# ScalarE takes the ordering reads, GpSimd all sums of the seventh and eighth tile, with new offsets in the planner

## The chip, the core and the metric

The kernel runs on one core of one Trainium2 chip, in one launch. The metric is device microseconds of one execution, as a median over runs. The core has TensorE (PE, the matrix engine), VectorE (DVE), ScalarE (ACT), GpSimd (POOL) and the queue engine SP, which issues most of the DMAs. Every engine works through its own queue strictly in order and waits on semaphores for what the others make.

## The reference

Two stages follow each other: a linear attention with decay in blocks of 64 positions, and a feed-forward layer with the gate h·cos(h).

```python
for b in range(nb):                                   # 12 blocks of 64
    intra = einsum('bhic,bhjc->bhij', qb, kb) * Dmask
    intra = einsum('bhij,bhjd->bhid', intra, vb)
    inter = einsum('bhid,bhde->bhie', qb * lam_pow, kv_state)
    out[:, :, sl] = intra + inter
    kv_state = lam_block * kv_state + einsum('bhsd,bhse->bhde', kb * rev_pow, vb)
x = out.transpose(0, 2, 1, 3).reshape(3072, 512)
h = x @ w_in                                          # 512 -> 2048
return (h * cos(h)) @ w_out                           # 2048 -> 512
```

Batch 4, 8 heads, 768 positions, head dimension 64; so the second stage has 3072 rows, which are 24 blocks of 128.

## The kernel before, in words

The 24 blocks are taken in pairs `pr`. The first two pairs (the spans) have a form of their own and make the lead of the kernel; each of the other ten pairs has one **visit** to TensorE: `add_scores` and `add_stretch` put down the scores (L458), the update of the state (L470), a first group of value matmuls (`values`, L521) and a second group with the carried state (`values_carried`, L521 and L553). Where two visits are joined, the scores and the update of the next pair stand between the two groups of values of this one. The two groups write into the same PSUM tiles from different row halves of the array; so that they are taken in turn, a one-element copy out of PSUM (`turn`, L538, seven of them) reads what the first group wrote, and the first matmul of the second group depends on it by hand (L547).

The feed-forward layer goes by nine tiles of 4, 2, 2, 2, 2, 4, 2, 2 and 4 blocks (`TILES`). For each slice of the hidden layer TensorE makes h (L828, or L1030 in the first four tiles), ScalarE its cosine (L834, L1036) and VectorE the product g (L837, L1042). The last five tiles (`FAST`, the fifth to the ninth) use a product scheme with seven instead of eight partial products; for that five sums of parts of g are made for each half of the slices (`combine`, L858, L860, L861: names 5, 2, 1, 7 and 6 for the halves 0 and 1, ten for a tile), and five sums of parts of w_out once (L786, on GpSimd, in twenty pieces, each held back until the values of a block named in `SLOT` are scaled). The products of a tile (L912, L909) run while the hidden layer of the next tile is made, and in the order of `SEQ`: for the first two blocks of a tile 5, 2, 3, 4, 1 of half 0, then 3, 4, 5, 2, 1 of half 1, then 7 and 6. The products 3 and 4 need no sum. VectorE joins the partial products to the output (L936, L946, L979), and SP stores it.

No order is written out by hand: a **planner** (`Planner.order`) places each task at build time, by given durations, latencies and buffers. On each engine it takes, of the tasks that could start first, the one with the smallest `prio`, and emits them in that order. A task with `worth` may be taken ahead of others although it could start that much later. `prio` is a due time: `begins` and `unit` are the planned starts and lengths of the tiles (`ATT` is what is added to them for each block), `LATER` moves the visits of a pair, `HASTE` the masks of the scores (L463) of pairs from 8 on, `CMB` and `CMBT` the sums of g (the latter by tile and half). `ON` names, for each tile, the engine of its ten sums: five of half 0, then five of half 1.

GpSimd also scales q and v (L380, L388) and casts k (L384) of all later blocks, as the loads land; SP then transposes q and k by DMA (L416).

Of the kernel before, what the change touches and what calls it, by code (L numbers as in the profile page):

```python
# [20 lines left out]
SPLIT = 5  # L21
BANKS = 8
LAG = 2
ATT = 0.95
LOAD_US = 1.22
ALONE = [3, 4, 8]
WF = ["ACT", "POOL", "ACT", "POOL"]
# [2 lines left out]
HELD = (10,) * 12  # L30
FAST = [4, 5, 6, 7, 8]
TILES = [4, 2, 2, 2, 2, 4, 2, 2, 4]
CMB = (-3.0, 5.0, -1.0)
HASTE = 10
CMBT = [(0.0, 0.0), (0.0, 0.0), (0.0, 0.0), (0.0, 0.0), (12.0, 12.0), (-12.0, -12.0), (16.0, 34.0), (0.0, -18.0), (6.0, -16.0)]
LATER = {3: 7.0, 4: -2.0, 5: -8.0, 6: -8.0, 7: -2.0, 8: 14.0, 9: 7.0, 10: 10.0, 11: 4.0}
KACT = ()
ON = ['DDDDDDDDDD', 'DDDDDDDDDD', 'DDDDDDDDDD', 'DDDDDDDDDD', 'DDDDDDDDDD', 'DDDDDDDDDD', 'PPPPPDDDDD', 'PPPPPDDDDD', 'DDDDDDDDDD']
SLOT = [5, 6, 6, 7, 8, 9, 9, 10, 10, 11, 11, 11, 12, 12, 12, 13, 13, 14, 15, 16]
WSUM = [(x, "POOL", 2, 70.0) for x in ("11+22", "12-22", "21-11", "21+22", "11+12")]  # L40
SEQ = [[(n, (g,)) for g, x in enumerate(("52341", "34521")) for n in x] + [(n, (0, 1)) for n in "76"], [(n, (0, 1)) for n in "5234176"]]

# [138 lines left out]
def kernel(  # L181
# [10 lines left out]
    nc = tc.nc  # L192
    B, H, S, D = q.shape
# [3 lines left out]
    NP = H // 2  # L197
# [55 lines left out]
    spare = consts.tile([P, 112], F32)  # L253
# [7 lines left out]
    pl = Planner({**BUFS, "q_f": BUFS["ld"], "k_f": BUFS["ld"], "v_f": BUFS["ld"]})  # L261
# [4 lines left out]
    live = {}  # L266

    HF, HM = KF // 2, DM // 2
    QF = HF // 2
    unit = [MM(n * P, 4 * KF) + (MM(HM, 7 * HF * n // 2) if i in FAST else MM(DM, KF * n)) + ATT * n for i, n in enumerate(TILES)]  # L270
    begins = [sum(unit[:i]) for i in range(len(unit) + 1)]

    def prio_attn(n, part):
        i = next(i for i in range(len(TILES)) if n < first[i + 1])
        return begins[i - 1] + unit[i - 1] * (n - n % 2 - first[i] + 2 * part) / TILES[i]
# [87 lines left out]
    def tile_of(n):  # L363
        return next((i, n - first[i]) for i in range(len(TILES)) if n < first[i + 1])
# [80 lines left out]
    def add_scores(pr, part):  # L445
# [38 lines left out]
        for s in range(2):  # L484
            So[n0 + s] = pl.add("DVE", 0.69, [s_t] + ([So[n0]] if s else []), partial(scores_out, s=s), pa(0.25 + 0.1 * s) - (HASTE if pr >= 8 else 0.0), get="s_m")
        s_t.bank_frees = [[So[n0]], [So[n0 + 1]]]
# [21 lines left out]
    def add_stretch(pr, ahead=None):  # L508


        n0 = 2 * pr
        g, c = divmod(pr, NB)
        pa = lambda part: prio_attn(n0, part)
        visit = pa(0.5) + LATER.get(pr, 0.0)
        tile_i, j0 = tile_of(n0)
# [19 lines left out]

        def turn(_):

            live["turn", pr] = nc.vector.tensor_copy(spare[D:D + 1, 0:1], live["o", n0][D:D + 1, NP - 1, D:D + 1])  # L538

        def values_carried(_):  # L540
            if not more and not apart and not ahead:
# [41 lines left out]
        if ahead:  # L583
            v1 = pl.add("PE", 4 * QUART + SW, [So[n0], So[n0 + 1]] + ahead.deps, values, ahead.prio, banks=2)
# [3 lines left out]
        else:  # L588
            v1 = pl.add("PE", 4 * QUART + SW * (1 if more else 2), deps, values, visit, banks=2 + 2 * apart)
# [4 lines left out]
                v1.deps += [d for d in t.deps if d not in nxt]  # L594
            chain += nxt
        if more or ahead:
            look = pl.add("DVE", 0.12, [v1], turn, pa(-9.0))
            look.worth = 0.45
            deps = deps + [look]
        v2 = v12[pr] = pl.add("PE", (12 if c else 8) * QUART + (SW if ahead else 0.0), deps, values_carried, visit)  # L600
# [173 lines left out]
    def add_w_sums():  # L774
# [14 lines left out]
        for k, (name, e, parts, prio) in enumerate(WSUM):  # L789
            for g in range(2):  # L790
                loaded = [w_t["out", 0], w_t["out", 2]] if g == 0 else [w_t["out", 1]] + w_last
                w_sum[name, g] = []
                for x in range(parts):
                    at = slice(x * QF // parts, (x + 1) * QF // parts)
                    slot = [d_t[SLOT[len(slots)]]] if len(slots) < len(SLOT) else []
                    slots.append(1)
# [11 lines left out]
    def add_fast_ffn(i):  # L808
# [54 lines left out]
        for g in range(2):  # L863
            ready = [gate[f + y] for f in range(QF * g, QF * g + QF) for y in (0, HF)]
            for k, name in enumerate("52176"):
                e = {"D": "DVE", "P": "POOL"}[ON[i][5 * g + k]]
                t = pl.add(e, 0.07 + np_ * QF * P / 1920.0 if e == "DVE" else 1.04 * np_, ready + ([sums[{"7": "5", "6": "2"}[name], g][0]] if name in "76" else []), partial(combine, name=name, g=g, e=e),
                           begins[i + 1] + CMB[0] + CMBT[i][g] + CMB[1] * k + CMB[2] * g, get="cmb" if name in "125" else None, lat=0.17)
                t.lock = e == "DVE"
# [270 lines left out]
    pr = SPANS  # L1140
    for i in range(len(TILES)):
        if i in FAST[:1]:
            add_w_sums()
        while 2 * pr < first[i + 1]:
            if pr + 1 in ALONE:
                add_scores(pr + 1, prio_attn(2 * pr + 2, 0.2))
            add_stretch(pr, first_update if pr == SPANS else None)
            pr += 1
        add_ffn(i)
# [99 lines left out]
```

## Time and profile before

| | us |
|---|---|
| median of 3 runs | 199.88 |
| lowest and highest | 199.56, 200.06 |
| the profiled execution | 198.76 |
| span of the profiled execution, first to last instruction | 196.7 |
| TensorE busy | 191.4 |
| VectorE busy | 143.1 |
| ScalarE busy | 112.3 |
| GpSimd busy | 99.9 |

The profiled execution lies 1.12 us below the median of the runs shown, and 2.06 us of it lie outside its span. TensorE's granted clock is 1.000 throughout. In the views a row of the timeline reads: start in us from the span's start, duration in us, engine, line, operation, output and inputs, shapes, how many were merged, and in brackets how long the engine was idle before and what ended that. PE rows are matmuls, PEld rows the weight loads that go with them; a matmul's record is longer than its turn in the array, as matmuls overlap.

### The profile page before, as it was taken

The page shows a single profiled execution, that of the slowest core. Times are in us where ns is not written, and L with a number is a line of the kernel's source. Part 1 is how long each engine was busy: PE and PEld are TensorE (multiplying, and loading weights), DVE is VectorE, ACT ScalarE, POOL GpSimd, SP SyncE. Part 2 cuts the span into 40 slices and gives each one's busy share as a digit, 9 for nine tenths or more (in the row PEclk, how much of TensorE's full clock was granted, in tenths as well). Part 3 has the DMA queues.
Part 4 walks back from the last instruction along what each step waited for, and adds up shares of the span by engine and source line. Part 5 has one row for each costly group of instructions (what it writes and reads, how often), then busy time and mean ns, then how long its engine had stood idle before and what let it go on. Part 6 is the DMA issues. An engine that isn't in the chain of part 4 may idle for free. (4 is left out here: it accounts for less than half of the span.)

```text
span 196.7 us, 6307 instructions
## 1 busy us (share of the span) xinstructions
PE 191.4 (97%) x2639; PEld 132.7 (67%) x2639; DVE 143.1 (73%) x273; ACT 112.3 (57%) x208; POOL 99.9 (51%) x116
## 2 busy tenths in 40 slices
PE   8999999999999999999999999999999999999993
PEld 3567544557748746867776545888888876456882
DVE  2979683448876934956877999996589775899933
ACT  4888871229868554928575686454246554865110
POOL 5794002287969899899584638106822850000000
PEclk9999999999999999999999999999999999999999
DMA  5999999999999999987999989696799201010133
GB/s 155 311 191 203 207 206 232 295 225 206 243 192 184 244 209 168 218 185 120 227 183 234 238 201 224 145 291 250 210 197 152 81 3 57 2 47 10 53 107 107
DMA packets 98685, 34.47 MB, mean 175 GB/s; under 512 B 84962, under 2 KB 96866, under 8 KB 98658
## 3 DMA queue, kind: packets, MB, share of 16 engines
q1 hardware_dynamic: 91680, 29.83, 70.3%
q0 software_dynamic: 6832, 4.20, 14.7%
q8 instruction: 20, 0.33, 0.7%
q10 hardware_dynamic: 146, 0.07, 0.1%
q14 instruction: 7, 0.06, 0.1%
HBM read 27.26 MB, written 6.29 MB: 171 GB/s over the span
## 5 line engine op out<-in xcount | busy, mean ns | idle before, releaser
L834 ACT ACTIVATE cos<-ps_h,halfpi 128x512 f32<-128x512 f32 x56 | 38.4, 688 | 27.9 <-PE ps_h L828 25.8
L828 PE MATMUL ps_h<-xT,w_in_sb 128*128 128x256 bf16 (+1 forms) x320 | 53.5, 315 | 0.0
L837 DVE TENSOR_TENSOR g<-ps_h,cos 128x512 bf16<-128x512 f32 x56 | 38.0, 688 | 10.6 <-ACT cos L834 10.0
L828 PEld LDWEIGHTS <-w_in_sb 128*128 128x128 bf16 x320 | 31.2, 98 | 15.1
L1042 DVE TENSOR_TENSOR g<-ps_h,cos 128x256 bf16<-128x256 f32 (+1 forms) x69 | 31.3, 467 | 8.7 <-ACT cos L1036 7.5
L1077 PE MATMUL ps_f<-w_out_sb,g 128*128 128x512 bf16 x160 | 37.5, 379 | 0.0
L1030 PE MATMUL ps_h<-xT,w_in_sb 128*128 128x256 bf16 (+1 forms) x276 | 36.2, 290 | 0.0
L1036 ACT ACTIVATE cos<-ps_h,halfpi 128x256 f32<-128x256 f32 (+1 forms) x69 | 32.3, 511 | 5.1 <-PE ps_h L1030 4.9
L380 POOL TENSOR_TENSOR qk<-q_f,q_scale 128x512 bf16<-128x512 f32 x19 | 20.4, 1084 | 25.4 <-DMA q_f<-in_q_dram 21.5
L1030 PEld LDWEIGHTS <-w_in_sb 128*128 128x128 bf16 x276 | 26.7, 98 | 8.8 <-DMA w_in_sb<-in_moe_w_in_dram 0.3
L388 POOL TENSOR_TENSOR v_s<-v_f,v_scale 128x512 bf16<-128x512 f32 x19 | 20.4, 1076 | 13.6 <-DMA v_f<-in_v_dram 12.7
L1077 PEld LDWEIGHTS <-g 128*128 128x128 bf16 x160 | 15.0, 98 | 15.3
L912 PEld LDWEIGHTS <-g 128*128 128x128 bf16 x208 | 20.1, 98 | 4.4 <-issue 0.3
L912 PEld LDWEIGHTS <-cmb 128*128 128x128 bf16 x168 | 16.1, 98 | 2.7
L561 ACT CAST xT<-ps_o 128x512 bf16<-128x512 f32 x15 | 8.1, 589 | 15.0 <-PE ps_o L553 12.6
L912 PE MATMUL ps_f<-w_out_sb,cmb 128*128 128x256 bf16 x112 | 15.0, 273 | 0.0
L463 DVE TENSOR_TENSOR s_m<-ps_s,mask 128x512 bf16<-128x512 f32 x20 | 12.9, 685 | 2.7 <-PE ps_s L458 2.3
L384 POOL CAST qk<-k_f 128x512 bf16<-128x512 f32 x18 | 11.5, 643 | 4.8 <-DMA k_f<-in_k_dram 4.6
L858 DVE TENSOR_TENSOR cmb<-g 128x512 bf16<-128x512 bf16 (+1 forms) x24 | 13.7, 600 | 0.3
L858 POOL TENSOR_TENSOR cmb<-g 128x512 bf16<-128x512 bf16 x6 | 6.8, 1155 | 10.5 <-PE ps_f L912 10.5
L476 DVE TENSOR_TENSOR sum<-sum,ps_kv 128x512 f32<-128x512 f32 x15 | 10.2, 683 | 0.6
L480 ACT CAST S<-sum 128x512 bf16<-128x512 f32 x15 | 9.1, 621 | 1.8 <-DVE sum L476 1.8
(109 smaller groups left out, 219.6 us busy)
## 6 DMA issues: line engine op xcount, KB each, us to landing
q_f<-in_q_dram SPq DMA_DIRECT2D x20, 256.0 KB, 3.7
k_f<-in_k_dram SPq DMA_DIRECT2D x20, 256.0 KB, 4.4
v_f<-in_v_dram SPq DMA_DIRECT2D x20, 256.0 KB, 4.4
out_dram<-o_sb SPq DMA_DIRECT2D x35, 128.0 KB, 1.8
w_out_sb<-in_moe_w_out_dram POOLq DMA_DIRECT2D x3, 512.0 KB, 13.3
out_dram<-o_sb SPq DMA_DIRECT2D x6, 256.0 KB, 2.7
sp_f<-in_q_dram SPq DMA_DIRECT2D x2, 512.0 KB, 4.9
sp_f<-in_k_dram SPq DMA_DIRECT2D x2, 512.0 KB, 5.0
```

What stands on the lines that cost most here:

```text
L380: return vec[e].tensor_mul(new_qk()[:, 0, :, s], live.pop(("q_f", 2 * pr + s)), q_scale[:, c, :].unsqueeze(2).to_broadcast([P, H, D]))
L388: return vec[e].tensor_mul(live["v_s", 2 * pr + s], live.pop(("v_f", 2 * pr + s)), v_scale[:, c, :].unsqueeze(2).to_broadcast([P, H, D]))
L463: return nc.vector.tensor_mul(t, live["s", pr][s], mask.unsqueeze(1).to_broadcast([P, H, D]))
L828: return [nc.tensor.matmul(t[:, x], lhsT=w_in_sb[:, kd, f * P:(f + 1) * P], rhs=live["xT", i][:, kd, :cols], start=(kd == 0), stop=(kd == ...
L834: return nc.scalar.activation(c, live["h", i, fs[0]], AF.Sin, bias=halfpi)
L837: return nc.vector.tensor_mul(g_tile()[:, fs[0]:fs[-1] + 1:HF, :cols], live.pop(("h", i, fs[0])), live.pop(("c", i, fs[0])))
L858: return v.tensor_add(c, *{"5": (a11, a12), "2": (a21, a22), "1": (a11, a22)}[name])
L912: return [nc.tensor.matmul(t, lhsT=left(name, f, p), rhs=right(what, f), start=(f % QF == 0 and opens is not None), stop=(f == HF - 1), sk ...
L1030: return [nc.tensor.matmul(t[:, :n], lhsT=w_in_sb[:, kd, f * P:(f + 1) * P], rhs=live["xT", i][:, kd, at], start=(kd == 0), stop=(kd == KD ...
L1036: nc.scalar.activation(c[:, :n], live["h", i, f, at.start][:, :n], AF.Sin, bias=halfpi)
L1042: return nc.vector.tensor_mul(live["g", i][:, f, at], live.pop(("h", i, f, at.start))[:, :n], live.pop(("c", i, f, at.start))[:, :n])
L1077: return [nc.tensor.matmul(live["f", i, j, piece][:, :width], lhsT=live["g", i][:, f, j * P:(j + 1) * P], rhs=w_out_sb[:, f, part], start= ...
```

## The change

The ordering read between the two groups of values is made by ScalarE instead of VectorE (`TURN`; the planner now gives it 0.2 us and 0.16 us until others see it). The five sums of half 1 of the seventh and the eighth tile, so far on VectorE, go to GpSimd, where those of half 0 are already. The planner's constants for due times are new: `ATT`, `CMB`, `HASTE`, `CMBT`, `LATER` and `SLOT`. What is computed, and by how many matmuls, stays.

```diff
-ATT = 0.95
+ATT = 1.4
-CMB = (-3.0, 5.0, -1.0)
-HASTE = 10
-CMBT = [(0.0, 0.0), (0.0, 0.0), (0.0, 0.0), (0.0, 0.0), (12.0, 12.0), (-12.0, -12.0), (16.0, 34.0), (0.0, -18.0), (6.0, -16.0)]
-LATER = {3: 7.0, 4: -2.0, 5: -8.0, 6: -8.0, 7: -2.0, 8: 14.0, 9: 7.0, 10: 10.0, 11: 4.0}
+CMB = (-8.0, 0.0, -6.0)
+HASTE = 15
+TURN = 'ACT'
+CMBT = [(0.0, 0.0), (0.0, 0.0), (0.0, 0.0), (0.0, 0.0), (30.0, 26.0), (6.0, -12.0), (24.0, 62.0), (42.0, -16.0), (0.0, 40.0)]
+LATER = {3: -8.0, 4: -4.0, 5: -2.0, 6: 4.0, 7: 14.0, 8: 7.0, 9: 10.0, 10: 14.0, 11: 0.0}
...
-ON = [..., 'PPPPPDDDDD', 'PPPPPDDDDD', 'DDDDDDDDDD']
-SLOT = [5, 6, 6, 7, 8, 9, 9, 10, 10, 11, 11, 11, 12, 12, 12, 13, 13, 14, 15, 16]
+ON = [..., 'PPPPPPPPPP', 'PPPPPPPPPP', 'DDDDDDDDDD']
+SLOT = [5, 5, 7, 7, 7, 8, 8, 9, 10, 10, 11, 11, 11, 12, 12, 12, 12, 15, 16, 18]
...
-            live["turn", pr] = nc.vector.tensor_copy(spare[D:D + 1, 0:1], live["o", n0][D:D + 1, NP - 1, D:D + 1])
+            live["turn", pr] = (nc.scalar.copy if TURN == "ACT" else nc.vector.tensor_copy)(spare[D:D + 1, 0:1], live["o", n0][D:D + 1, NP - 1, D:D + 1])
...
-            look = pl.add("DVE", 0.12, [v1], turn, pa(-9.0))
+            look = pl.add(TURN, 0.2 if TURN == "ACT" else 0.12, [v1], turn, pa(-9.0), lat=0.16)
             look.worth = 0.45
```

More of the change, by code (lines that the diff above doesn't have):

```diff
@@ L32 @@
 TILES = [4, 2, 2, 2, 2, 4, 2, 2, 4]
-CMB = (-3.0, 5.0, -1.0)
-HASTE = 10
-CMBT = [(0.0, 0.0), (0.0, 0.0), (0.0, 0.0), (0.0, 0.0), (12.0, 12.0), (-12.0, -12.0), (16.0, 34.0), (0.0, -18.0), (6.0, -16.0)]
-LATER = {3: 7.0, 4: -2.0, 5: -8.0, 6: -8.0, 7: -2.0, 8: 14.0, 9: 7.0, 10: 10.0, 11: 4.0}
+CMB = (-8.0, 0.0, -6.0)
[3 more added lines that the diff above has]
+LATER = {3: -8.0, 4: -4.0, 5: -2.0, 6: 4.0, 7: 14.0, 8: 7.0, 9: 10.0, 10: 14.0, 11: 0.0}
 KACT = ()
-ON = ['DDDDDDDDDD', 'DDDDDDDDDD', 'DDDDDDDDDD', 'DDDDDDDDDD', 'DDDDDDDDDD', 'DDDDDDDDDD', 'PPPPPDDDDD', 'PPPPPDDDDD', 'DDDDDDDDDD']
-SLOT = [5, 6, 6, 7, 8, 9, 9, 10, 10, 11, 11, 11, 12, 12, 12, 13, 13, 14, 15, 16]
+ON = ['DDDDDDDDDD', 'DDDDDDDDDD', 'DDDDDDDDDD', 'DDDDDDDDDD', 'DDDDDDDDDD', 'DDDDDDDDDD', 'PPPPPPPPPP', 'PPPPPPPPPP', 'DDDDDDDDDD']
+SLOT = [5, 5, 7, 7, 7, 8, 8, 9, 10, 10, 11, 11, 11, 12, 12, 12, 12, 15, 16, 18]
 WSUM = [(x, "POOL", 2, 70.0) for x in ("11+22", "12-22", "21-11", "21+22", "11+12")]
```

## The prediction

> **What bounds the kernel now.** I read the page's first part, then the busy times by stretch (stretch, its length, busy us and count of PE, PEld, DVE, ACT, POOL, granted clock, DMA share, GB/s), then TensorE's rows in the timeline, looking for places where a matmul starts later than the one before it allows.
>
> ```profile
> span 196.7 us, 6307 instructions
> ...
> PE 191.4 (97%) x2639; PEld 132.7 (67%) x2639; DVE 143.1 (73%) x273; ACT 112.3 (57%) x208; POOL 99.9 (51%) x116
> ```
>
> ```profile
> 0.00:15.00 15.00, 13.61 (x183) 7.82 (x184) 9.57 (x20) 10.59 (x23) 11.56 (x25) 1.00 1.17 218
> 15.00:105.00 90.00, 89.90 (x1327) 59.31 (x1325) 60.43 (x122) 56.86 (x115) 59.61 (x64) 1.00 1.10 209
> 105.00:125.00 20.00, 19.84 (x292) 11.30 (x291) 18.27 (x33) 13.27 (x21) 12.00 (x12) 1.00 1.01 220
> ...
> 145.00:165.00 20.00, 19.75 (x352) 17.06 (x346) 16.60 (x33) 10.55 (x19) 8.43 (x8) 1.00 0.55 78
> 165.00:187.00 22.00, 21.98 (x142) 13.65 (x141) 19.61 (x33) 12.06 (x18) 0.00 (x0) 1.00 0.11 37
> 187.00:196.70 9.70, 6.31 (x72) 5.67 (x71) 3.31 (x10) 0.59 (x1) 0.00 (x0) 1.00 0.32 108
> ```
>
> TensorE bounds it. It is idle for 5.3 us (196.7 − 191.4), and 4.8 of these lie in the lead (15.00 − 13.61 = 1.4) and at the end (9.70 − 6.31 = 3.4), which hold neither an ordering read nor one of the moved sums. Number and kind of matmuls stay, so the change can only win or lose **stalls** between 15 and 187 us. Part of a stall is hidden in busy time, because a matmul's record runs on while the next could start; so I take them from the starts. I find four that matter. The first is at 123 us:
>
> ```profile
> 121.28 2.49 POOL L388 TENSOR_TENSOR v_s<-v_f,v_scale 128x512 bf16<-128x512 f32 x2 [0.71 <-DMA v_f<-in_v_dram]
> ...
> 121.82 1.05 DVE L860 TENSOR_TENSOR g<-g 128x1024 bf16<-128x1024 bf16 x1
> ...
> 122.80 0.68 DVE L837 TENSOR_TENSOR g<-ps_h,cos 128x512 bf16<-128x512 f32 x1
> ...
> 123.15 0.21 PE L470 MATMUL ps_kv<-v_s,qk 64*64 64x64 bf16 x1
> ...
> 123.50 0.16 DVE L538 COPY spare<-ps_o 1x1 f32<-1x1 f32 x1
> 123.53 0.44 PE L470 MATMUL ps_kv<-v_s,qk 64*64 64x64 bf16 x31 [0.16 <-DVE g L837]
> ```
>
> The update of the state (L470) issues one matmul at 123.15 and the next at 123.53. At the pace of its others (31 in 0.44 us) it would have been some 0.01 later, so **0.37 us** are lost. It waits for VectorE's g, ended at 123.48, which stood behind a sum that took 1.05 us beside GpSimd's work. The second is near the end:
>
> ```profile
> 185.07 1.91 PE L912 MATMUL ps_f<-w_out_sb,cmb 128*128 128x256 bf16 x16
> 185.08 0.69 DVE L861 TENSOR_TENSOR g<-g 128x1024 bf16<-128x1024 bf16 x1
> 185.69 0.75 DVE L936 TENSOR_TENSOR E<-ps_f,SA 128x256 f32<-128x256 f32 x2
> 186.35 0.68 DVE L946 TENSOR_TENSOR o_sb<-ps_f,SA 128x512 f32<-128x512 f32 x1
> ...
> 187.09 1.03 PE L912 MATMUL ps_f<-w_21+22_1759,g 128*128 128x256 bf16 x8
> ```
>
> Sixteen matmuls in 1.91 us with the last one's record of 0.27 (eight take 1.03) are 0.109 from start to start, so the next could start at 185.07 + 16 × 0.109 = 186.82; it starts at 187.09, behind VectorE's L861, L936 and L946: **0.27 us**. The other two name no engine:
>
> ```profile
> 103.21 0.74 PE L521 MATMUL ps_o<-s_m,v_s 64*64 64x64 bf16 x32
> 103.77 0.43 PE L553 MATMUL ps_o<-qkT,S 64*64 64x64 bf16 x32
> ```
>
> ```profile
> 161.21 0.43 PE L553 MATMUL ps_o<-qkT,S 64*64 64x64 bf16 x25
> 161.89 0.25 PE L553 MATMUL ps_o<-qkT,S 64*64 64x64 bf16 x7 [0.25 <-issue]
> ```
>
> The visit at 103 is a single one, and the code drains TensorE between its groups (L542): 32 matmuls take 0.74 instead of some 0.45, **0.3 us**. At 161, 32 take from 161.21 to 162.14, 0.93 against 0.43: **0.5 us** whose cause no row gives. Together 1.4 us, 0.7% of the time, and only the first two (0.64) have VectorE, which the change relieves, in front of them.
>
> **The ordering reads.**
>
> ```profile
> L682 ACT CAST kv_bd<-ps_kv 64x256 bf16<-64x256 f32 x4 | 1.5, 370 | 0.0
> ...
> L538 DVE COPY spare<-ps_o 1x1 f32<-1x1 f32 x7 | 1.1, 156 | 8.9 <-PE ps_o L521 8.9
> ...
> L1187 ACT ACTIVATE lnl<-ps_lam 128x8 f32<-128x8 f32 x1 | 0.2, 177 | 0.8 <-PE ps_lam L1185 0.8
> ```
>
> ```profile
> 98.90 0.32 PE L521 MATMUL ps_o<-s_m,v_s 64*64 64x64 bf16 x16
> 99.01 0.59 ACT L1093 COPY o_sb<-ps_f 128x512 f32<-128x512 f32 x1 [0.17 <-PE ps_f L1077]
> ...
> 99.28 0.16 DVE L538 COPY spare<-ps_o 1x1 f32<-1x1 f32 x1 [1.12 <-PE ps_o L521]
> ...
> 99.62 0.34 PE L521 MATMUL ps_o<-s_m,v_s 64*64 64x64 bf16 x16
> ```
>
> VectorE loses seven reads of 156 ns (1.1 us) and the wait ahead of them (8.9 us of idle time, most of it with nothing else to do). ScalarE gets seven. No row shows this read on ScalarE; the shortest row there that reads PSUM is 177 ns for eight columns, and below it nothing but zero bounds the read, above it the next shape that reads PSUM, 0.37 us. I take 0.18, so 1.3 us of ScalarE, which has 84 us idle. For TensorE what counts is when the read ends. At 99 us it ends at 99.44 and the second group starts at 99.62; scores and update lie between. So up to **0.18 us** of slack, of which a ScalarE read 0.02 longer uses little: at its best the move costs TensorE nothing. Without this cover it would cost the seven reads whole, 1.3 us. Behind a waiting read on ScalarE stand the next cosine and, after the second group, the copies to xT (L561), which wait for that group anyway; a cosine held back by the read's 0.3 to 0.4 us delays g and a PSUM bank by as much, while TensorE is in the visit.
>
> **The sums.** Ten instructions leave VectorE and ten go to GpSimd.
>
> ```profile
> L858 DVE TENSOR_TENSOR cmb<-g x24: 417/680/1266, 95.2 to 183.9; 128x512 bf16<-128x512 bf16 x12, 128x1024 bf16<-128x1024 bf16 x12
> L858 POOL TENSOR_TENSOR cmb<-g x6: 1152/1156/1158, 134.3 to 156.6; 128x512 bf16<-128x512 bf16 x6
> ```
>
> These are 128x512: 0.42 us each on VectorE, so 4.2 us at least, and 1.16 on GpSimd, so 11.6 us. GpSimd can take them: it is busy 8.4 of 20 us in 145 to 165 and not at all after. Their DMAs are none; but on GpSimd's queue they stand among the scaling of v and the casts of k for the last pair, each of which can come one sum (1.16) later.
>
> ```profile
> 153.38 1.04 POOL L388 TENSOR_TENSOR v_s<-v_f,v_scale 128x512 bf16<-128x512 f32 x1 [4.55 <-DMA v_f<-in_v_dram]
> ...
> 158.83 1.16 POOL L861 TENSOR_TENSOR g<-g 128x512 bf16<-128x512 bf16 x1
> ...
> 161.10 1.10 DVE L858 TENSOR_TENSOR cmb<-g 128x512 bf16<-128x512 bf16 x3
> ...
> 163.83 0.60 PE L912 MATMUL ps_f<-w_out_sb,cmb 128*128 128x256 bf16 x4
> ```
>
> ```profile
> 172.90 0.60 PE L912 MATMUL ps_f<-w_out_sb,cmb 128*128 128x256 bf16 x4
> ```
>
> The last scaling of v ends at 154.4, and the last visit reads the carried state at 161.21 (above): some 6 us cover the delay. The eighth tile is the tight one. Its second half is ready at 161.1; on GpSimd the five sums end at 162.3, 163.4, 164.6, 165.7 and 166.9. TensorE asked for the first at 163.83 and for the second at 172.90, with the ninth tile's hidden layer between; so all five are in time where that order stays. Cost zero, and VectorE's gain of 4.2 us reaches TensorE only at a stall, of which there is none due to it between 125 and 165.
>
> The Trainium skill ("SBUF — State Buffer", § Who interferes with whom) says that a VectorE instruction with two SBUF inputs and a GpSimd instruction that reads SBUF shut each other out for the whole instruction. The spread from 417 to 1266 ns above agrees. By this rule the moved sums would hold up no g, as that reads PSUM and one SBUF input, and the sum stays as it is.
>
> **The offsets.** They permute the queues. TensorE is fed in every stretch, so a new order neither saves nor adds a matmul; it sets which meetings such as that of 121.8 us occur. Bounds: all four stalls gone (−1.4) and, on the other side, as much again (+1.4). I take the nearest row: the stall of 123 us, a chance meeting of one sum and one scaling of v, goes (−0.37). The one at 187 stays: the sums of the last tile are still on VectorE, and after the last g there they follow one another whatever their due times.
>
> **Sum.** −0.37 (first stall) + 0 (reads) + 0 (sums) = −0.37 on the profiled 198.76, so 198.4; the median of the runs is 1.12 above that execution, so **199.5**.
>
> **The rivals.**
> 1. Faster: the stall at 187 and the unnamed one go too, −0.37 − 0.27 − 0.5 = −1.14, so 198.7. For it: VectorE is busy 19.61 of 22 us in 165 to 187, and the sums of half 0 there get an earlier due time (`CMB`). Against: the sums of half 1, of which L861 above ends last (185.77), can't start before the last g.
> 2. Slower: **the reads come late in ScalarE's queue.** At 99 us ScalarE was in a copy until 99.60, when the read was due at 99.28; and it starts a cosine in two other visits:
>
> ```profile
> 122.86 0.69 ACT L834 ACTIVATE cos<-ps_h,halfpi 128x512 f32<-128x512 f32 x1 [0.61 <-PE ps_h L828]
> ```
>
> ```profile
> 158.03 0.69 ACT L834 ACTIVATE cos<-ps_h,halfpi 128x512 f32<-128x512 f32 x1 [1.50 <-PE ps_h L828]
> 158.29 0.16 DVE L538 COPY spare<-ps_o 1x1 f32<-1x1 f32 x1 [1.04 <-PE ps_o L521]
> ```
>
> Behind these the reads would be 0.32, 0.42 (due at 122.75 + 0.38, as at 99) and 0.43 late. It decides from 0.18 us on; with the slack used up they cost 0.14 + 0.24 + 0.25 = 0.6, without any slack 1.2. Taking 0.9, with nothing won: 200.8. Against it: the planner may put the read ahead by 0.45 us.
> 3. Slower: **the sums on the path.** The Trainium skill ("GPSIMD Engine Reference", § 4.1 Engine selection) advises VectorE for elementwise additions, with GpSimd about twice as slow; the rows here say 2.8 times (1156 to 417). If TensorE takes all products of the eighth tile ahead of the ninth's hidden layer, which follows the product of 163.83 at 164.3 (four starts of 0.109 on), it waits for the last sum at 166.9: up to +2.6, so 202.5. Against it: the 6 us of other work between the two products above.
> 4. The offsets bring one meeting for another and nothing changes: 199.9.
>
> **How the numbers follow.** A measurement of this kernel can tell about 0.3%, 0.6 us, from no change. Chances: the forecast 0.36, no change 0.08, rival 1 0.33, rival 2 0.15, rival 3 0.08. So faster by over 0.3% 0.33, within 0.44, slower 0.23. The range holds the forecast, no change, and rivals 1 and 2 at their values: 198.7 to 200.9; outside lie rival 3 and the edges of the other two, together some 0.2.
>
> **What would show it.** Right: ScalarE's read rows near 0.18 us, the second group 0.72 us after the first as at 99 us, no wait of TensorE on g inside a visit, GpSimd's twenty sums at 1.16 and TensorE without idle time between 161 and 170. Wrong: a second group that starts over 0.9 us after the first with ScalarE's row ending just before it (rival 2); a wait of L912 on GpSimd (rival 3); the gaps at 161 or 187 gone (rival 1); or a lead longer or shorter than now, which I hold fixed.

## The result, and the profile after

The changed kernel is faster: its median is 198.46 us over six runs (197.61 to 199.10) against 199.57 for the kernel before over six (199.44 to 200.06). The ratio is 0.9938, with a 95% interval from 0.9910 to 0.9966. The forecast was 199.5, in a range that began at 198.7; it took 0.37 off a median of 199.88, and over six runs the measured difference of the medians is 1.11. In the experiments below, single executions far off the rest (202.59 us in offsets_only, 391.31 in after_read_on_vector, 495.79 in sums_alone) count in the medians and not in the ratios.

| us | before | after |
|---|---|---|
| median of six runs | 199.57 | 198.46 |
| the profiled execution | 198.76 | 197.61 |
| its span | 196.7 | 195.9 |
| the rest, outside the span | 2.06 | 1.71 |

The first thing to see is the last row: of the 1.15 us between the two profiled executions only 0.8 lie inside the span. The other 0.35 stand in no view; the section on the hardware comes back to them.

The page's first part and the busy times by stretch of the changed kernel, in the columns that the prediction explains (every line number of the kernel's body is one higher than before):

```profile
span 195.9 us, 6308 instructions
...
PE 190.9 (97%) x2639; PEld 132.9 (68%) x2639; DVE 139.0 (71%) x256; ACT 113.6 (58%) x215; POOL 109.5 (56%) x126
```

```profile
0.00:15.00 15.00, 13.39 (x181) 7.71 (x182) 9.39 (x20) 10.42 (x22) 11.38 (x25) 1.00 1.16 218
15.00:105.00 90.00, 89.90 (x1327) 59.51 (x1326) 60.64 (x119) 57.67 (x119) 58.61 (x64) 1.00 1.11 210
105.00:125.00 20.00, 20.00 (x294) 11.56 (x293) 17.80 (x30) 14.26 (x24) 11.97 (x13) 1.00 0.99 212
125.00:145.00 20.00, 20.00 (x243) 17.79 (x242) 15.60 (x27) 7.64 (x13) 9.26 (x9) 1.00 0.86 245
145.00:165.00 20.00, 20.00 (x411) 17.50 (x401) 12.44 (x21) 11.39 (x21) 17.98 (x18) 1.00 0.35 80
165.00:187.00 22.00, 22.00 (x142) 13.75 (x141) 19.82 (x33) 12.08 (x18) 0.32 (x1) 1.00 0.07 25
187.00:195.90 8.90, 5.61 (x68) 5.05 (x65) 3.27 (x9) 0.08 (x1) 0.00 (x0) 0.98 0.35 118
```

From 105 us to 187 us TensorE has no idle time left; before, it had 0.16 in the stretch up to 125, 0.25 in that up to 165 and 0.02 after. The lead costs 1.61 instead of 1.39 and the end 3.29 instead of 3.39. The work has moved as the diff says: VectorE is 4.1 us less busy and GpSimd 9.6 us more; the stretch from 145 to 165 us alone accounts for that (16.60 to 12.44, and 8.43 to 17.98), and the other stretches about cancel.

The two costs that the prediction could only bound, in the groups of the changed kernel by shape (busy us, mean ns of one, idle time before):

```profile
L859 POOL TENSOR_TENSOR cmb<-g 128x512 bf16<-128x512 bf16 x12 | 13.6, 1157 | 15.0 <-DVE g L838 15.0
...
L539 ACT COPY spare<-ps_o 1x1 f32<-1x1 f32 x7 | 1.1, 150 | 9.1 <-PE ps_o L522 9.1
```

ScalarE's read takes 150 ns (0.18 was taken, VectorE's took 156), and GpSimd's sums 1.157 us, as forecast.

At the visit that lost 0.37 us at 123 us before, two sums stood ahead of the g besides the one at 121.82:

```profile
119.38 0.72 DVE L858 TENSOR_TENSOR cmb<-g 128x1024 bf16<-128x1024 bf16 x1
...
120.62 0.68 DVE L858 TENSOR_TENSOR cmb<-g 128x1024 bf16<-128x1024 bf16 x1
```

In the timeline of the changed kernel the same visit begins at 120.26:

```profile
117.56 0.68 DVE L859 TENSOR_TENSOR cmb<-g 128x1024 bf16<-128x1024 bf16 x1
...
119.78 0.69 DVE L838 TENSOR_TENSOR g<-ps_h,cos 128x512 bf16<-128x512 f32 x1 [0.34 <-ACT cos L835]
120.26 0.32 PE L522 MATMUL ps_o<-s_m,v_s 64*64 64x64 bf16 x16
...
120.63 0.15 ACT L539 COPY spare<-ps_o 1x1 f32<-1x1 f32 x1 [0.88 <-PE ps_o L522]
120.66 0.60 PE L471 MATMUL ps_kv<-v_s,qk 64*64 64x64 bf16 x32
...
121.08 0.34 PE L522 MATMUL ps_o<-s_m,v_s 64*64 64x64 bf16 x16
```

Of the three sums, one now stands ahead of the visit's g, at 117.56, and it takes its 0.68 us. VectorE even waits 0.34 us for the cosine. The 32 matmuls of L471 come in one row, and the second group starts 0.82 us after the first.

The end of the last tile, first before, VectorE's last g (L837) and the sums behind it, then after:

```profile
181.95 0.69 DVE L837 TENSOR_TENSOR g<-ps_h,cos 128x512 bf16<-128x512 f32 x1
182.67 1.90 DVE L858 TENSOR_TENSOR cmb<-g 128x1024 bf16<-128x1024 bf16 x3
```

```profile
180.41 1.34 DVE L838 TENSOR_TENSOR g<-ps_h,cos 128x512 bf16<-128x512 f32 x2
181.86 1.90 DVE L859 TENSOR_TENSOR cmb<-g 128x1024 bf16<-128x1024 bf16 x3
...
184.51 1.91 PE L913 MATMUL ps_f<-w_out_sb,cmb 128*128 128x256 bf16 x16
...
185.56 0.68 DVE L947 TENSOR_TENSOR o_sb<-ps_f,SA 128x512 f32<-128x512 f32 x1
186.30 1.03 PE L913 MATMUL ps_f<-w_21+22_1558,g 128*128 128x256 bf16 x8
```

From the start of the sixteen matmuls to the start of the next eight it is now 186.30 − 184.51 = 1.79 us, where it was 187.09 − 185.07 = 2.02 with the stall of 0.27. VectorE's sums begin 184.51 − 181.86 = 2.65 us ahead of the sixteen; before, it was 185.07 − 182.67 = 2.40. So VectorE had come **0.25 us late out of its last g**, and no longer does: two g that take 1.34 instead of the usual 1.28 suggest that it has caught up and waits a little for the cosine.

### The profile page after: what moved, and what is told of

It reads as the page before. It is cut to its first block, busy times and chain, and to the rows that moved or that the text cites. A ratio compares the mean times of both kernels' runs of the same rounds, so it can differ in the third digit from the quotient of the medians.

```text
span 195.9 us, 6308 instructions
## 1 busy us (share of the span) xinstructions
PE 190.9 (97%) x2639; PEld 132.9 (68%) x2639; DVE 139.0 (71%) x256; ACT 113.6 (58%) x215; POOL 109.5 (56%) x126
## 4 chain that ended last, share of the span: by engine, by line
PE 93%; DMA 3%; SPq 1%; POOL 1%; issue 0%; DVE 0%; POOLq 0%
PE ps_h L829 25%; PE ps_f L913 21%; PE ps_f L1078 18%; PE ps_h L1031 18%; DMA sp_f<-in_k_dram 3%; PE ps_o L522 2%; PE ps_s L459 2%; PE ps_o L554 2%; PE ps_kv L471 2%; SPq L290 1%; PE ps_f L910 1%; PE ps_o L692 1%; PE ps_kv L679 1%; POOL k_sp L647 1%; PE ps_t L411 0%; PE ps_t L655 0%
## 5 line engine op out<-in xcount | busy, mean ns | idle before, releaser
L829 PE MATMUL ps_h<-xT,w_in_sb 128*128 128x256 bf16 (+1 forms) x320 | 52.8, 315 | 0.0
L1031 PE MATMUL ps_h<-xT,w_in_sb 128*128 128x256 bf16 (+1 forms) x276 | 36.0, 290 | 0.0
L381 POOL TENSOR_TENSOR qk<-q_f,q_scale 128x512 bf16<-128x512 f32 x19 | 19.8, 1057 | 24.7 <-DMA q_f<-in_q_dram 22.1
L389 POOL TENSOR_TENSOR v_s<-v_f,v_scale 128x512 bf16<-128x512 f32 x19 | 19.8, 1044 | 5.9 <-DMA v_f<-in_v_dram 5.8
L859 POOL TENSOR_TENSOR cmb<-g 128x512 bf16<-128x512 bf16 x12 | 13.6, 1157 | 15.0 <-DVE g L838 15.0
L464 DVE TENSOR_TENSOR s_m<-ps_s,mask 128x512 bf16<-128x512 f32 x20 | 12.9, 684 | 9.6 <-PE ps_s L459 9.6
L859 DVE TENSOR_TENSOR cmb<-g 128x1024 bf16<-128x1024 bf16 (+1 forms) x18 | 10.5, 620 | 0.3
```

The costliest lines, as they stand in the source:

```text
L381: return vec[e].tensor_mul(new_qk()[:, 0, :, s], live.pop(("q_f", 2 * pr + s)), q_scale[:, c, :].unsqueeze(2).to_broadcast([P, H, D]))
L389: return vec[e].tensor_mul(live["v_s", 2 * pr + s], live.pop(("v_f", 2 * pr + s)), v_scale[:, c, :].unsqueeze(2).to_broadcast([P, H, D]))
L464: return nc.vector.tensor_mul(t, live["s", pr][s], mask.unsqueeze(1).to_broadcast([P, H, D]))
L829: return [nc.tensor.matmul(t[:, x], lhsT=w_in_sb[:, kd, f * P:(f + 1) * P], rhs=live["xT", i][:, kd, :cols], start=(kd == 0), stop=(kd == ...
L859: return v.tensor_add(c, *{"5": (a11, a12), "2": (a21, a22), "1": (a11, a22)}[name])
L1031: return [nc.tensor.matmul(t[:, :n], lhsT=w_in_sb[:, kd, f * P:(f + 1) * P], rhs=live["xT", i][:, kd, at], start=(kd == 0), stop=(kd == KD ...
```

## The experiments

Stalls are read as in the prediction, from the starts of TensorE's matmuls. "Span" is the median span of a kernel's runs as a difference to that of the kernel before on the same chip (197.4 to 197.7), and "outside" the mean of time minus span (the kernel before: 2.08 to 2.10).

| kernel | offsets | reads | half-1 sums | median us | ratio to before (95%) | span | outside |
|---|---|---|---|---|---|---|---|
| offsets_only | new | VectorE | VectorE | 199.43 | 0.9993 (0.9972 to 1.0013) | +0.1 | 1.72 |
| read_alone | old | ScalarE | VectorE | 198.68 | 0.9963 (0.9942 to 0.9984) | −0.75 | 2.06 |
| sums_alone | old | VectorE | GpSimd | 199.31 | 0.9977 (0.9948 to 1.0006) | −0.2 | 2.04 |
| moves_only | old | ScalarE | GpSimd | 198.27 | 0.9920 (0.9901 to 0.9939) | −1.0 | 1.71 |
| moves_only_again | old | ScalarE | GpSimd | 198.12 | 0.9936 (0.9910 to 0.9961) | −0.95 | 1.69 |
| after_without_read | new | VectorE | GpSimd | 198.66 | 0.9945 (0.9927 to 0.9964) | −1.1 | 2.08 |
| after_without_sums | new | ScalarE | VectorE | 199.40 | 0.9991 (0.9972 to 1.0011) | −0.1 | 1.79 |
| after_again | new | ScalarE | GpSimd | 198.31 | 0.9942 (0.9922 to 0.9963) | −0.8 | 1.73 |

The planner places every task anew when one cost or constant is changed. So two kinds of experiment are needed: those of the table, in which the plan is made anew, and those in which the plan stays as it was and one instruction is emitted on another engine.

**The offsets without the moves, and the moves without the offsets.** The first theory was that the new order makes the gain, the second that it is VectorE's relief.

```diff
 # offsets_only: the changed kernel with
-ON = [..., 'PPPPPPPPPP', 'PPPPPPPPPP', 'DDDDDDDDDD']
+ON = [..., 'PPPPPDDDDD', 'PPPPPDDDDD', 'DDDDDDDDDD']
 # and the ordering reads, with their costs in the planner, as before
```

> The new offsets alone; the ordering reads and the half-1 sums of tiles seven and eight stay on VectorE. Theory A (the new order of the queues did it): the stalls at 123, 161 and 187 us are gone here too, 0.8 to 1.1 us faster than before, ratio 0.9945 to 0.996. Theory B (VectorE relieved of reads and sums did it): those offsets alone leave VectorE as full as before, at least two of the three stalls stay, ratio 0.998 to 1.003.

```diff
 # moves_only: the changed kernel with ATT, CMB, HASTE, CMBT, LATER and SLOT as before
-ATT = 1.4
+ATT = 0.95
...
```

> The reads on ScalarE and the sums on GpSimd, with the offsets of before. Theory A: stalls of the same size as before at other places, ratio 0.998 to 1.003. Theory B: the stalls that VectorE caused (0.37 at 123, 0.27 at 187) go, ratio 0.995 to 0.997. Rival 2 of the prediction (reads late behind ScalarE's work): second groups of values over 0.9 us after the first in two or three visits, ratio 1.003 to 1.006.

The offsets alone give nothing, the moves alone give all of the gain. Yet the offsets do remove the stall at 123 us; a new one takes its place. The timeline of offsets_only from 160 us:

```profile
160.24 1.09 DVE L859 TENSOR_TENSOR cmb<-g 128x512 bf16<-128x512 bf16 x3
...
161.25 0.42 DVE L861 TENSOR_TENSOR g<-g 128x512 bf16<-128x512 bf16 x1
...
161.59 0.42 DVE L862 TENSOR_TENSOR g<-g 128x512 bf16<-128x512 bf16 x1
...
161.93 1.28 DVE L464 TENSOR_TENSOR s_m<-ps_s,mask 128x512 bf16<-128x512 f32 x2
...
164.14 0.32 PE L522 MATMUL ps_x<-s_m,v_s 64*64 64x64 bf16 x16
...
166.03 0.81 PE L829 MATMUL ps_h<-xT,w_in_sb 128*128 128x512 bf16 x2 [1.12 <-ACT xT L571]
```

The five sums of the eighth tile's second half stand on VectorE ahead of the masks (L464) of the last visit. So the visit starts at 164.14 only, after the products that TensorE could have taken behind it, and the hidden layer of the ninth tile waits 1.12 us for xT. The same place in the changed kernel, whose sums of that half are on GpSimd:

```profile
162.07 0.32 PE L522 MATMUL ps_x<-s_m,v_s 64*64 64x64 bf16 x16
...
162.82 0.61 PE L913 MATMUL ps_f<-w_21-11_1485,g 128*128 128x256 bf16 x4
...
163.27 1.04 PE L913 MATMUL ps_f<-w_out_sb,cmb 128*128 128x256 bf16 x8
...
164.14 0.60 PE L913 MATMUL ps_f<-w_11+22_755,cmb 128*128 128x256 bf16 x4
...
164.58 1.67 PE L829 MATMUL ps_h<-xT,w_in_sb 128*128 128x512 bf16 x7
```

The visit is two microseconds earlier in the order, and sixteen matmuls of the products lie between it and the hidden layer while xT is made. Nothing waits.

**One instruction on the other engine, the plan unchanged.** First in the plan of the changed kernel:

```diff
 # after_read_on_vector: the plan of the changed kernel; only the emission
-            live["turn", pr] = (nc.scalar.copy if TURN == "ACT" else nc.vector.tensor_copy)(spare[...], ...)
+            live["turn", pr] = nc.vector.tensor_copy(spare[...], ...)
```

> The plan of the changed kernel held fixed, every queue in its order, but the seven reads emitted on VectorE at their planned places. Theory A: as the changed kernel, ratio 0.993 to 0.9955. Theory B: reads stand behind a g of 0.69 us in VectorE's queue at one to three visits, each 0.2 to 0.5 us for TensorE, so 0.4 to 1.0 us slower than the changed kernel, ratio 0.996 to 0.999.

```diff
 # after_sums_on_vector: the plan of the changed kernel; the ten half-1 sums are emitted on VectorE
-    partial(combine, name=name, g=g, e=e)
+    partial(combine, name=name, g=g, e="DVE" if g and i in (6, 7) else e)
```

> The plan of the changed kernel held fixed, but the ten half-1 sums of tiles seven and eight emitted on VectorE at their planned places (0.42 us each instead of 1.16 on GpSimd). Theory A: as the changed kernel, ratio 0.993 to 0.9955. Theory B: VectorE gets 4.2 us back between 144 and 165, stands in front of TensorE there, 0.3 to 0.8 us slower than the changed kernel, ratio 0.9955 to 0.998.

With the read on VectorE the kernel takes 199.47 us, 0.9983 of before (0.9966 to 1.0000): most of the gain is gone. A part of that, some 0.35 us, lies outside the span, where this kernel takes 2.08 us and the changed one 1.72; its span is still 0.3 us shorter than before's. For the part inside, see its timeline at 159 us:

```profile
159.25 0.32 PE L522 MATMUL ps_o<-s_m,v_s 64*64 64x64 bf16 x16
...
159.53 0.68 DVE L838 TENSOR_TENSOR g<-ps_h,cos 128x512 bf16<-128x512 f32 x1
...
160.24 0.16 DVE L539 COPY spare<-ps_o 1x1 f32<-1x1 f32 x1
...
160.46 0.32 PE L522 MATMUL ps_o<-s_m,v_s 64*64 64x64 bf16 x16 [0.36 <-DVE spare L539]
```

The read stands behind a g that ends at 160.21, and the second group starts 1.21 us after the first instead of 0.7. A second visit, at 99.6 us, is late by as much, some 0.53 us each. In the plan of the changed kernel the read belongs on ScalarE. The sums do not need GpSimd in this plan: 198.40 us, 0.9937 (0.9917 to 0.9958), as fast as the changed kernel. There the masks of the last visit keep their place ahead of the sums, because the plan still believes the sums to be on GpSimd. (Outside the span this kernel takes 1.81 us.) So it is not VectorE's 4.2 us that count but **where in its queue they stand**.

Then in the plan of the kernel before:

```diff
 # before_read_on_scalar: the plan of before (its planner line too); only the emission
-            live["turn", pr] = nc.vector.tensor_copy(spare[...], ...)
+            live["turn", pr] = nc.scalar.copy(spare[...], ...)
```

> The plan of the kernel before held fixed, but the seven reads emitted on ScalarE at their planned places. The prediction's price: read of 0.18 us with up to 0.18 us of slack, so no cost by itself. Theory A: the stalls at 123 (0.37) and 187 (0.27) stay, ratio 0.999 to 1.001. Theory B: less waiting in VectorE's queue, ratio 0.997 to 0.999. Rival 2: behind cosines and a copy at 99, 123 and 158 us, 0.6 to 1.2 us slower, ratio 1.003 to 1.006.

```diff
 # before_sums_on_gpsimd: the plan of before; the ten half-1 sums are emitted on GpSimd
-    partial(combine, name=name, g=g, e=e)
+    partial(combine, name=name, g=g, e="POOL" if g and i in (6, 7) else e)
```

> The plan of the kernel before held fixed, but the ten half-1 sums of tiles seven and eight emitted on GpSimd at their planned places. Theory A: no stall of before was due to these sums, ratio 0.999 to 1.001, unless products asked for at 151 to 156 and 163.83 us come before their sum (rival 3), then up to 1.005. Theory B: 4.2 us less on VectorE, ratio 0.997 to 0.999.

Both come out at no change: 199.53 us, 0.9997 (0.9978 to 1.0015), and 199.51, 0.9995 (0.9975 to 1.0015). In the first, rival 2 of the prediction can be seen, in the timeline at 158.9 us:

```profile
158.91 0.32 PE L522 MATMUL ps_o<-s_m,v_s 64*64 64x64 bf16 x16
159.02 0.69 ACT L835 ACTIVATE cos<-ps_h,halfpi 128x512 f32<-128x512 f32 x1 [1.50 <-PE ps_h L829]
...
159.73 0.15 ACT L539 COPY spare<-ps_o 1x1 f32<-1x1 f32 x1
...
159.94 0.32 PE L522 MATMUL ps_o<-s_m,v_s 64*64 64x64 bf16 x16 [0.18 <-ACT spare L539]
```

ScalarE had begun a cosine; the read waits for it, and the second group starts 1.03 us after the first, some 0.35 late. At 100 us it is 0.18. Against that stands the stall at 123, which these two profiles show at 0.90 and 1.12 us, far above the 0.37 of the first profile of before. That difference asked for the next experiments.

**One move with the plan made anew.**

```diff
 # read_alone: the kernel before with the ScalarE read and its planner line
+TURN = 'ACT'
-            look = pl.add("DVE", 0.12, [v1], turn, pa(-9.0))
+            look = pl.add(TURN, 0.2 if TURN == "ACT" else 0.12, [v1], turn, pa(-9.0), lat=0.16)
```

> The read on ScalarE alone, with a new plan from the old offsets and the sums as before. Theory A: ratio 0.998 to 1.003, stalls at other places. Theory B: 0.997 to 0.999.

```diff
 # sums_alone: the kernel before with
-ON = [..., 'PPPPPDDDDD', 'PPPPPDDDDD', 'DDDDDDDDDD']
+ON = [..., 'PPPPPPPPPP', 'PPPPPPPPPP', 'DDDDDDDDDD']
```

> The ten sums on GpSimd alone, with a new plan from the old offsets and the reads on VectorE. Theory A: the order up to 125 us is that of before, the stall at 123 stays, ratio 0.998 to 1.002. Theory B: 0.997 to 0.999.

The timeline of sums_alone at the visit of 123 us, where the order of before is kept:

```profile
119.64 1.52 DVE L859 TENSOR_TENSOR cmb<-g 128x1024 bf16<-128x1024 bf16 x1
...
120.55 1.63 POOL L385 CAST qk<-k_f 128x512 bf16<-128x512 f32 x2
...
121.68 1.04 DVE L859 TENSOR_TENSOR cmb<-g 128x1024 bf16<-128x1024 bf16 x1
...
122.41 2.67 POOL L389 TENSOR_TENSOR v_s<-v_f,v_scale 128x512 bf16<-128x512 f32 x2 [0.23 <-DMA v_f<-in_v_dram]
...
123.25 0.93 DVE L861 TENSOR_TENSOR g<-g 128x1024 bf16<-128x1024 bf16 x1
...
123.41 0.21 PE L471 MATMUL ps_kv<-v_s,qk 64*64 64x64 bf16 x1
...
124.83 0.44 PE L471 MATMUL ps_kv<-v_s,qk 64*64 64x64 bf16 x31 [1.21 <-DVE g L838]
```

Three sums stand ahead of the g, and each of them takes longer than 0.68 us: 1.52, 1.04 and 0.93, together 1.45 too long. The stall is 1.39. GpSimd's work beside them stretches too: two casts take 1.63 us, two scalings 2.67. In read_alone the new plan puts two sums of 0.68 and L980 ahead of that g, and TensorE doesn't wait there; its span is 0.75 us shorter, and its ratio is below what either theory had expected. So the read moved alone wins, by the order that comes of it and not by itself: in the plan of before it won nothing.

**Is the stall at 123 us a meeting of VectorE's sums with GpSimd?** Over the profiles that keep the order of before, the stall is what the three sums take over 3 × 0.68, less some 0.05:

| kernel | three sums over 2.04 us | stall at 123 us |
|---|---|---|
| before, first profile | 0.41 | 0.35 to 0.37 |
| before_no_meeting | 0.53 | 0.49 |
| before_again | 0.61 | 0.56 |
| before_read_on_scalar | 0.95 | 0.90 |
| before_sums_on_gpsimd | 1.16 | 1.12 |
| sums_alone | 1.45 | 1.39 |
| before_shifted (further below) | 0.55, and 0.75 of a fourth sum | 1.17 |

In the last one a sum at 116.63 already takes 1.43 us, beside two scalings of q; with its 0.75 the four are 1.30 too long.

To test it, GpSimd's work there was left out, with the plan of before, and fills with a constant put in its place:

```diff
 # before_no_meeting: for blocks 20 and 21, v scaling and k cast (prep_v, prep_k)
+            if 2 * pr + s in (20, 21):
+                nc.gpsimd.tensor_copy(spare[0:1, ...], live.pop(("v_f", 2 * pr + s))[0:1, 0, 0:1])
+                return nc.gpsimd.memset(live["v_s", 2 * pr + s], 0.01)
 # before_no_meeting_q: the same in prep_q too
```

> The plan of the kernel before, every queue in its order; GpSimd's scaling of v and cast of k for the blocks 20 and 21 (117 to 124 us) are left out and each replaced by a copy of one element, which waits for the same load, and a fill that reads nothing. Lock theory (VectorE's sums wait while GpSimd reads SBUF, and TensorE waits for the g behind them): sums of 0.67 to 0.70 us between 117 and 124, stall of L470 at 123 under 0.1, 0.6 to 1.1 us faster than before, ratio 0.9945 to 0.997. Load theory (VectorE simply has too much to do there): the stall stays at 0.3 or more, ratio 0.998 to 1.002.

> As before_no_meeting, with GpSimd's scaling of q for the blocks 20 and 21 left out in the same way. In the kernels with the plan of before, the stall at 123 us was the sum of what three VectorE sums between 119 and 123 us took over 0.68 us, less 0.06 (0.41 and 0.35; 0.61 and 0.56; 0.53 and 0.49; 1.16 and 1.12). Lock theory: all three at 0.67 to 0.69, stall under 0.05, ratio 0.995 to 0.998. Load theory: a stall of 0.3 or more with sums of 0.68.

before_no_meeting gives 198.92 us, 0.9980 (0.9965 to 0.9995), and still has one long sum, of 1.23 us, beside the scaling of q that was left. With that gone too, the timeline of before_no_meeting_q reads (its lines are up to nine further than in before):

```profile
119.59 0.68 DVE L867 TENSOR_TENSOR cmb<-g 128x1024 bf16<-128x1024 bf16 x1
...
120.79 0.68 DVE L867 TENSOR_TENSOR cmb<-g 128x1024 bf16<-128x1024 bf16 x1
...
121.99 0.68 DVE L869 TENSOR_TENSOR g<-g 128x1024 bf16<-128x1024 bf16 x1
...
123.36 0.49 PE L479 MATMUL ps_kv<-v_s,qk 64*64 64x64 bf16 x32
```

All three sums take 0.68, and the 32 matmuls go without a gap. The fills of 0.51 us that GpSimd makes there instead read nothing, and they stretch no sum. The kernel takes 198.89 us, 0.9953 (0.9937 to 0.9969), its span is 0.9 us shorter. **Without the meeting the kernel of before is 0.9 us faster in the median**, with an interval from 0.6 to 1.3. (The two medians, 198.92 and 198.89, are hardly apart, but from chips on which the kernel before has 199.44 and 199.80; the intervals of the two ratios just overlap.) In the last profile the stalls at 161 and 187 us are still there (0.53 and 0.27). The changed kernel's span is shorter by nearly as much (0.8), but from more terms than this one; they are added up below. The rule that the prediction named from the Trainium skill ("SBUF — State Buffer", § Who interferes with whom), that such a sum and a GpSimd instruction that reads SBUF shut each other out, agrees with these rows: the sums stretch where GpSimd works beside them and not where that work is gone.

**How much of it is chance of one execution.** The kernel before, moves_only and the changed kernel ran a second time:

> The kernel before once more, unchanged, for a second profile. If the stall at 123 us varies with the moment at which GpSimd's scaling of v meets VectorE's sum, it is another size than the 0.37 us of the first profile: 0.9 to 1.4 as in the kernels that kept that plan. If it is fixed by the plan, it is 0.3 to 0.5 again.

> The reads on ScalarE and the sums on GpSimd with the offsets of before, a second time, beside the changed kernel on the same chip. If the offsets add nothing to the moves: ratio 0.991 to 0.995, the interval overlapping the changed kernel's. If the first result was by chance: 0.995 to 0.998. The profile tells whether the stall at 123 us (0.95 in the first profile) is the rule there.

> The changed kernel a second time on the same chip as moves_only_again. Ratio 0.992 to 0.996; no stall over 0.3 us other than the drain near 103 us.

The kernel before shows 0.56 at 123 us this time; moves_only, which in its first profile (the slowest of its seven runs, 199.51 us) had a stall of 0.95 there, has none; the changed kernel again has none there, but 0.33 at 163 us, which it was not expected to have. GpSimd's scalings start when loads land, so the same program meets more or less of them.

**The changed kernel with one move taken back, the plan made anew.**

```diff
 # after_without_read: the changed kernel with the read and the planner line of before
-TURN = 'ACT'
+TURN = 'DVE'
 # after_without_sums: the changed kernel with the ON of before
```

> The changed kernel without the move of the reads, planned anew: offsets and sums of after, reads on VectorE. If the read on ScalarE is worth 0.5% with these offsets whatever the plan (late reads behind a g at 99 and 159 us, 0.53 each, as with the plan held fixed): ratio 0.997 to 0.9995. If a new plan finds places for them on VectorE: 0.993 to 0.996.

> The changed kernel without the move of the sums, planned anew: offsets and reads of after, half-1 sums of tiles seven and eight on VectorE. If the sums matter only through the plan (offsets_only waited 1.2 us for xT at 164.7): 0.994 to 0.998 with that wait or without; if they do not matter: 0.992 to 0.995.

Without the ScalarE read the plan is as good: 0.9945 against 0.9938 and 0.9942, with no late read. Without GpSimd's sums the stall of 1.12 us for xT is back, and the gain is gone.

**The unnamed stall at 161 us.** Its cause had no row, and from the starts of the matmuls it is 0.42 us, not 0.5. If it belonged to the place in the stream of TensorE's instructions rather than to the work, more instructions ahead of it would move it:

```diff
 # before_shifted: the kernel before with 32 small idle matmuls more in the lead
     ones_of(4 * P, F32)
+    for _ in range(32):
+        ones_of(D)
```

> The kernel before with 32 more small matmuls in the lead, which feed nothing: TensorE's stream of instructions is shifted by 64. The stall of 0.42 us inside L553 at 161.4, twice the same in the kernel before, has no wait on a semaphore. If it hangs on the place in the instruction stream, it is gone or another size (a change of over 0.15); if on what the other engines do at that time, it stays at 0.4.

At 161 us nothing of that size is left; there is 0.13 at 163.43, inside L521 and no longer inside L553. In its timeline another gap without a releaser has come up, inside a product (four matmuls that belong together):

```profile
148.22 0.27 PE L912 MATMUL ps_f<-w_21-11_1546,g 128*128 128x256 bf16 x1
...
148.70 0.50 PE L912 MATMUL ps_f<-w_21-11_1546,g 128*128 128x256 bf16 x3 [0.21 <-issue]
```

From start to start it is 0.48 us where 0.11 is usual, and no semaphore is waited for. The packed trace does hold something that fits: the packets of the queue q8, which the page lists as instructions, 20 of 16 KB in every profile and 21 in before_shifted, whose TensorE has 64 instructions more. So they are taken here for TensorE's own instructions.

| profile | 18th packet of q8, from and to | the matmul behind the gap starts | gap |
|---|---|---|---|
| before | 159.18, 160.52 | 161.89 | 0.42 |
| before_no_meeting | 159.92, 161.34 | 162.78 | 0.87 |
| before_sums_on_gpsimd | 160.30, 161.26 | 162.65 | 0.17 |
| moves_only_again | 159.08, 160.21 | 161.78 | 0.53 |
| the changed kernel | 159.83, 161.27 | 162.54 | 0.09 |
| the changed kernel, second profile | 160.45, 162.05 | 163.33 | 0.33 |

In all fourteen profiles that have the gap, besides before_shifted, TensorE goes on 1.2 to 1.6 us after that packet has landed, and wherever all 2639 matmuls have a row it is one of the 2397th to 2400th, whatever the kernel. The gap at 148.70 ends 1.42 us after the 16th packet has landed, at 147.28. So **the unnamed stall looks like TensorE waiting for its next instructions**. In the changed kernel it comes to that place later after the start of the fetch: it had 2.6 us, and before 2.3 (161.47 − 159.18). No run changed the fetches alone, so this is a fit of times and not a test.

Of all versions, none ran faster than the changed kernel beyond the interval; moves_only is equal.

## Why the prediction was wrong

The miss of 1.04 us has three parts of about equal size. The median of three runs from which the forecast started, 199.88, lay 0.31 above the median of six. The time outside the span fell by 0.35, which no term had. And inside the span the change is worth some 0.75 where 0.37 was forecast. The steps, in the order of the prediction:

- **TensorE as the bound, the number of matmuls, and stalls as the only place to win: right** for the span. That 0.35 us could come from outside the span was not thought of.
- **The reads at nothing: right** as a cost by themselves. In the plan of before the move is worth 0.03% with an interval of ±0.19%, and in the changed kernel taking it back with a new plan costs nothing that can be told (its span is even some 0.3 shorter, which the longer time outside the span takes back). The read took 0.15 us.
- **Rival 2, reads late behind a cosine: real, but not in this plan.** In the plan of before the two late reads cost 0.18 and 0.35 us on TensorE, where 0.14 and 0.25 had been worked out, and the third was covered by the stall at 123. In neither profile of the changed kernel is a read late: all seven start as soon as TensorE's first group lets them, after idle time of ScalarE. The planner knows ScalarE's queue, as the prediction's "against" had it.
- **The first stall goes: right. Its size, −0.37: wrong**, and this is the term that was mis-sized most. It was measured in one execution, and that one lay 1.12 us below the median of the runs. The prediction saw this and carried the 1.12 over as a constant. A part of it was the median of only three runs. Another was the very stall that the change removes: 0.35 to 1.12 in the plan of before, 0.9 in the median by before_no_meeting_q. With −0.9 on the median, 199.88, the sum would have been 198.98.
- **"The one at 187 stays": wrong.** The step argued that the sums of the last tile follow one another after the last g, whatever their due times. They do, but the last g itself came 0.25 us late out of a queue that VectorE had been working through without a break since 172.9. In the changed kernel the joining of the eighth tile (L937, L947) is done at 165.02 instead of 174.70, and VectorE has caught up before its last g. That isn't the only way: moves_only_again keeps the joining at 174.76, orders sums and g differently, and has no stall either (1.78 from the sixteen to the eight). Of the plans made anew, only read_alone, with the old offsets and the sums on VectorE, keeps the 0.27.
- **"VectorE's gain of 4.2 us reaches TensorE only at a stall, of which there is none due to it between 125 and 165": right for the order of before, wrong for the change.** The moves and the offsets were costed one by one. The new offsets would have made such a stall, 1.12 us for xT behind five sums, and it is the plan made for sums on GpSimd that keeps it out: new offsets planned with the sums on VectorE give 0.9993 and 0.9991, with the sums on GpSimd 0.9945 and 0.9938, and 0.9937 where they are planned for GpSimd and emitted on VectorE.
- **Rival 1 (the stalls at 187 and the unnamed one go too, 198.7) came nearest**, and its mechanism is what the first pair of profiles shows: all three stalls go. That its number lies only 0.24 above the result is partly luck. It started from a median 0.31 too high and did not have the 0.35 outside the span, and the unnamed stall is back with 0.33 in the changed kernel's second profile.
- **Rival 3 (sums on the path) did not come**: no product waits for GpSimd, and TensorE has no idle time from 105 to 187 us.

Added up for the first pair of profiles, matmul by matmul (each has 2639, so that the n-th of one can be set against the n-th of the other): the changed kernel is 0.02 us behind at the 250th (22.7 us), so its longer lead is made up by then, and 0.11 behind at the 1500th (104 us). It is 0.18 ahead at the 2200th (156 us), behind the visit of the first stall; 0.56 ahead at the 2500th (178 us), behind the unnamed one; and 0.79 ahead at the 2600th (189 us), behind that of 187. That is the span's −0.8. For the medians, −0.9 for the meeting and −0.25 for the end would be −1.15, where −0.8 to −1.0 is measured (the changed kernel and moves_only); what makes up the rest was not tested. One pair of executions says little about it: the second profiles of the two kernels differ by 0.2 us in span only (196.9 and 196.7), as the changed kernel's lead was 0.4 us longer in its second profile than in its first. Outside the span come another −0.35, whose cause is open.

## What to carry to other kernels

When one profiled execution lies well off the median, the stall you mean to remove may be what differs between them: size it from several executions, or from the instruction that stretches (here a sum of 0.68 us that took up to 1.52), not from the one row. Where a planner places the work, parts of a change can't be added up one by one; ask of each new order which instruction now stands ahead of the one that TensorE waits for next. Moving work off an engine that isn't the bound pays by the place it frees in a queue, not by the microseconds moved.

## What the runs showed of the hardware

- A VectorE sum of 128x1024 bf16 takes 0.68 us alone and up to 1.52 beside GpSimd's scalings and casts, and these stretch too (two casts 1.63 us instead of some 1.2, two scalings 2.67 instead of 2.04). Which side is stretched differs: in read_alone a sum begun at 120.83 kept its 0.68, and the pair of casts beside it took 1.72.
- A one-element read of PSUM takes ScalarE 150 ns and VectorE 156 ns; in these runs, who makes it matters through what it stands behind.
- In the profiles with the gap at 161 to 163 us, TensorE goes on 1.2 to 1.6 us after a packet of 16 KB of instructions has landed, at the same place of its stream in all kernels, and loses up to 0.87 us. The place lies in a visit, whose matmuls are short (32 in 0.43 us), so that TensorE soon comes to the instructions of the next packet; that this is why it waits there is an inference.
- The time outside the span depends on the program. It is 2.08 to 2.10 us for the kernel before on four chips, 1.69 to 1.73 for moves_only and the changed kernel, 1.72 for offsets_only, and each kernel keeps its value within ±0.07 from run to run (between lie before_sums_on_gpsimd at 1.95, after_sums_on_vector at 1.81 and after_without_sums at 1.79). The last rows inside the span, the issue of the last store, before and after:

```profile
193.76 0.38 ACTq L987 DMA_DIRECT2D out_dram<-o_sb  x1
```

```profile
192.97 0.38 ACTq L988 DMA_DIRECT2D out_dram<-o_sb  x1
```

From the end of that issue to the end of the span it is 2.56 us (196.7 − 194.14) and 2.55 (195.9 − 193.35), so the 0.35 us lie before the first record or after the last. offsets_only and moves_only both have the shorter time and share no part of the change; after_without_read and after_read_on_vector, with 2.08, don't have it. What it depends on stays open.
